# A decode attention block whose keys are scored three ways: 32 of a tile's 256 positions by TensorE's transposes, none summed by ScalarE, and VectorE's multiplication in two parts

## The chip, the cores and the metric

The kernel runs on one core of one Trainium2 chip. The metric is the device time of one execution in microseconds (us). It was run three times: 668.6, 667.44 and 668.81 us, so the median is 668.6 us. One more execution, recorded by the hardware profiler, took 667.49 us; its span, from the first to the last instruction, is 665.8 us. All durations below are from that execution.

## What is computed

One decode step of a transformer block for two sequences: layer norm, attention over a cache of 8,192 positions in 32 heads of 128 elements, and a gated layer behind it. Nearly all bytes are the two caches, 2 x 32 x 8,192 x 128 bf16 values each.

```
q = layernorm(x) @ wq                                   # 2 x 32 heads x 128
scores = einsum("bhqd,bhkd->bhqk", q, k) * 128 ** -0.5  # k: 2 x 32 x 8192 x 128
o = einsum("bhqk,bhkd->bhqd", softmax(scores), v)
h = x + o.reshape(2, 1, 4096) @ wo
out = h + glu(layernorm(h))                             # W_gate, W_up, W_down
```

## The kernel before

**Tiles.** There are 16 steps (`N`), one for four heads of one sequence. Partition 32 j + r of a step holds 256 consecutive positions of head j, so a tile of keys, K(i), is 128 partitions x 256 positions x 128 elements, 8.39 MB, and a tile of values, V(i), is laid out alike. A "position" below is one of the 256 in each partition. There are three such buffers. `load_v(i)` writes V(i) into the buffer that held K(i), once that tile's scores are finished, and `load_k(i + 1)` writes into the buffer of V(i - 2), once the value products of step i - 2 are done. All these loads are issued on SyncE's queue, in the order V(i - 1), K(i + 1), V(i), K(i + 2) and so on (L145).

**The scores of a tile** (`scores`, L331) are made in three ways:
- By VectorE: `mult` (L341) multiplies positions in place by the query, repeated over the partitions. Then the 128 products of each position are added in halves, 128 to 64, 32, 16 and 8 (L412), and a last reduction adds the 8 (L416).
- By ScalarE: `sum_up` (L345 to L350) takes positions that VectorE has multiplied and adds up each one's 128 products, one activation with an accumulator for each position (`NACT`: 48 a tile, 32 in the last).
- By TensorE: `transposed` (L352) transposes 8 positions at a time, and `by_columns` (L359) has ScalarE copy them from PSUM to the tile `kT` (L362) and then multiplies each with the query columns (L364). There is one `kT`, and there are two PSUM tiles for transposed keys, so the transposes of the third chunk follow the products of the first. `scores_of` (L372) copies these scores into the column tile. `NPE` is the number of these positions: none in the first tile, 16 in a middle one, 32 in the last.

**Softmax and values.** `best(i)` (L310) reduces the scores of each partition to their maximum and spreads it with a matmul on TensorE (L314). `powers(i)` (L319) reduces that to the negative maximum on VectorE (L323, tile `nm`) and then has ScalarE make four exponentials (L326) into `pgz`, the weights for the values. It is called in the middle of `scores(i + 1)`. `values(i)` (L433) multiplies `pgz` with V(i): two matmuls written out (L427), and then a loop of 31 rounds of two matmuls each on TensorE (L451 to L453) for the steps 0 to 12. The steps 13 to 15 are written out. `collect` (L461) copies the result of a loop, and `turn` (L469) turns the results of four steps at a time.

**What sets the order.** The order on TensorE, VectorE, ScalarE and SyncE is that of the program text (`manual_schedule`). In a middle step, VectorE multiplies 16 positions (`FIRST`), then 176 (`MIDDLE`), makes the negative maximum of the step before, multiplies the last 48, and adds. ScalarE sums 16 positions, copies the value product of step i - 2, copies two chunks of transposed keys, makes the exponentials of step i - 1, copies the column scores and sums 32 positions. TensorE transposes 16 positions, makes their products and then runs the loop of step i - 1. The first loop's head is placed on slot 169 of an instruction block (`LOOP_AT`, L450); the later ones stand where the code between them puts them.

**The end.** When the scores of the last tile are done, the output and gated-layer weights are loaded into its buffer (L500 to L518), behind the two halves of V(15) in the queue. The rest of the block follows.

Of the kernel before, what the change touches and what calls it, by code (L numbers as in the profile page):

```python
# [7 lines left out]
ACT = mybir.ActivationFunctionType  # L8
ALU = mybir.AluOpType
AXIS = mybir.AxisListType  # L10
# [3 lines left out]
def _free(t, offset, dims):  # L14

    return bass.AP(tensor=t.tensor, offset=t.offset + offset, ap=[t.ap[0]] + [list(d) for d in dims])
# [7 lines left out]
def kernel(  # L24
# [13 lines left out]
    nc = tc.nc  # L38
    P = nc.NUM_PARTITIONS
    B, Sq, D = A_x.shape  # L40
    _, Hkv, Sk, Dh = A_k_cache.shape
# [6 lines left out]
    NT = H4 * Sk // P  # L48
# [2 lines left out]


    TPC = 8
    FIRST = 16
    MIDDLE = 176
    T4 = 4

# [8 lines left out]
    f32 = mybir.dt.float32  # L66
# [19 lines left out]
    ps = ctx.enter_context(tc.tile_pool(name="ps", bufs=1, space=PSUM))  # L86
# [7 lines left out]
    N = len(steps)  # L94
# [40 lines left out]
    hc = consts.tile([P, B, KC], f32)  # L135

    COLS = N - 3
    NACT = {i: 32 if i == N - 1 else 48 for i in range(N)}
    NPE = {i: 0 if i == 0 else 32 if i == N - 1 else 16 for i in range(N)}

    def load_kv(cache, t, i, pieces=1):
        b, g = steps[i]
# [27 lines left out]
    with tc.manual_schedule(engines=ORDERED):  # L170
# [42 lines left out]
        for c in range(KC):  # L213
            nc.tensor.matmul(
                out=x_ps[:, c, :], lhsT=xrow[0:B, bass.DynSlice(c, P, step=KC)], rhs=ident[0:B, 0:B],
# [13 lines left out]
            out=xn.rearrange("p c b -> p b c"), in0=dev, in1=_free(rstd, 0, [[1, B], [0, KC]]), op=ALU.mult,  # L229
# [101 lines left out]
        def scores(i):  # L331
            b, g = steps[i]
            last = i == N - 1
            kt = buf[k_at[i]]
            nmul = NT - NPE[i]
            na = NACT[i]
            scol = scols[i] = small.tile([P, NT], f32, tag=f"scol{i % 2}", name="scol")

            def mult(t0, t1):
                kv = _free(kt, t0 * Dh, [[Dh, t1 - t0], [1, Dh]])  # L340
                nc.vector.tensor_tensor(  # L341
                    out=kv, in0=kv, in1=_free(qrep[b], g * Dh, [[0, t1 - t0], [1, Dh]]), op=ALU.mult,
                )

            def sum_up(t0, t1):  # L345
                for t in range(t0, t1):
                    whole = ps.tile([P, Dh], f32, tag="acc", name="whole")
                    nc.scalar.activation(  # L348
                        out=whole, in_=kt[:, t * Dh:(t + 1) * Dh], func=ACT.Copy, accum_out=scol[:, t:t + 1],
                    )  # L350

            def transposed(c0):  # L352
                t_ps = ps2.tile([P, TPC, P], bf16, tag="tp", name="t_ps")
                for k in range(TPC):
                    t = nmul + c0 + k
                    nc.tensor.transpose(t_ps[:, k, :], kt[:, t * Dh:(t + 1) * Dh], ident)  # L356
                return t_ps

            def by_columns(t_ps):  # L359
                sc_ps = ps.tile([P, NPE[i], H4], f32, tag="sc", name="sc_ps")  # L360
                for c0 in range(0, NPE[i], TPC):
                    nc.scalar.activation(out=kT, in_=t_ps.pop(0).rearrange("p t s -> p (t s)"), func=ACT.Copy)  # L362
                    for t in range(TPC):
                        nc.tensor.matmul(  # L364
                            out=sc_ps[:, c0 + t, :], lhsT=kT[:, t * P:(t + 1) * P],
                            rhs=_free(qT, H4 * g * B + b, [[B, H4]]), start=True, stop=True,
                        )
                    if c0 + 2 * TPC < NPE[i]:
                        t_ps.append(transposed(c0 + 2 * TPC))
                return sc_ps  # L370

            def scores_of(sc_ps):  # L372
                for j in range(H4):
                    r = slice(j * QP, (j + 1) * QP)
                    nc.scalar.activation(out=scol[r, nmul:NT], in_=sc_ps[r, :, j], func=ACT.Copy)  # L375

            left = []
            if i == 0:
                for t0 in range(0, NT, NT // 4):
                    mult(t0, t0 + NT // 4)  # L380
                sum_up(0, na)
            elif last:
                mult(0, nmul)
                scores_of(by_columns([transposed(c0) for c0 in (0, TPC)]))
                sum_up(0, na)
                values(i - 1)
            else:
                mult(0, FIRST)
                if i == 1:
                    powers(i - 1)  # L390
                mult(FIRST, FIRST + MIDDLE)
                t_ps = [transposed(c0) for c0 in (0, TPC)]
                sum_up(0, FIRST)
                if i >= 2:
                    collect(i - 2)
                sc_ps = by_columns(t_ps)
                if i >= 2:
                    powers(i - 1)
                    turn(i - 2)
                left = waiting[:]  # L400
                values(i - 1)
                tc.no_sync_barrier()
                load_k(i + 1)
                scores_of(sc_ps)
                mult(FIRST + MIDDLE, nmul)
                sum_up(FIRST, na)
            n = nmul - na
            width = Dh
            while width > 8:
                half = width // 2  # L410
                lo = _free(kt, na * Dh, [[Dh, n], [1, half]])
                nc.vector.tensor_tensor(  # L412
                    out=lo, in0=lo, in1=_free(kt, na * Dh + half, [[Dh, n], [1, half]]), op=ALU.add,
                )
                width = half
            nc.vector.tensor_reduce(  # L416
                out=scol[:, na:nmul], in_=_free(kt, na * Dh, [[Dh, n], [1, 8]]), axis=AXIS.X, op=ALU.add,
            )
            for e in left:
                waiting.remove(e)  # L420
                normalise(e)
            best(i)
# [10 lines left out]
        def values(i):  # L433
            v = buf[v_at[i]]
            if i >= COLS:
                sums(i)
                g = steps[i][1]
                for t in range(NT):
                    nc.tensor.matmul(  # L439
                        out=o_of(i)[:, 0, H4 * g:H4 * (g + 1)],  # L440
                        lhsT=v[:, t * Dh:(t + 1) * Dh], rhs=pgz[:, H4 * t:H4 * (t + 1)],
                        start=(t == 0), stop=(t == NT - 1),
                    )
                return

            made[i] = ps.tile([P, T4 * Dh], f32, tag="po", name="po")
            with tc.tile_critical(sync_engine=PE):  # L447
                products(i, 0, LOOP)

                at = {PE: LOOP_AT} if i == 0 else None  # L450
                with nc.Fori(1, NT // T4 // LOOP, 1, engines=[PE], head_slot=at) as w:  # L451
                    for u in range(LOOP):
                        nc.tensor.matmul(  # L453
                            out=made[i][0:H4 * T4, :],
                            lhsT=pgz[:, bass.ds((w * LOOP + u) * (H4 * T4), H4 * T4)],
                            rhs=v[:, bass.ds((w * LOOP + u) * (T4 * Dh), T4 * Dh)],
                            start=False, stop=True, skip_group_check=True,
                        )
# [36 lines left out]
        for (h0, m, blocks, k, loads), n in zip(SETS, rows):  # L495
            r0 = h0 * Dh
            for p0, w in blocks:
                r = 0
                for nr in loads:
                    nc.sync.dma_start(  # L500
                        out=wo_sb[p0:p0 + w, off + r * D:off + (r + nr) * D],
                        in_=_dram(A_wo, (r0 + r) * D, [[n * D, w], [1, nr * D]]),
# [9 lines left out]
        for w in WD:  # L512
            nc.sync.dma_start(  # L513
                out=wd2[:, k0:k0 + w, :],
                in_=_dram(B_W_down, k0 * 2 * P * D, [[2 * D, P], [2 * P * D, w], [1, 2 * D]]),
# [12 lines left out]
        for k, (h0, m, blocks, _, _) in enumerate(SETS):  # L528
            n = rows[k]
# [3 lines left out]
            for b in range(B):  # L533
# [4 lines left out]
                for p0, w in blocks:  # L538
                    mb = w // q
                    nc.vector.tensor_tensor(  # L540
                        out=_free(sp, p0, [[q, mb], [1, q]]), in0=_free(ocol, h1 * B + b, [[B, mb], [0, q]]),
                        in1=_free(quot[k], 0, [[0, mb], [1, q]]), op=ALU.mult,
# [4 lines left out]
        for k, (h0, m, blocks, _, _) in enumerate(SETS):  # L547
            n = rows[k]
            pn = sum(blocks[-1])
            for r in range(n):  # L550
                for c in range(KC):
                    nc.tensor.matmul(
                        out=att_ps[:, c, :],
# [18 lines left out]
            out=hx, in0=_free(hc, 0, [[1, KC], [KC, B], [0, PARTS]]), in1=_free(part, 0, [[0, KC], [0, B], [1, PARTS]]),  # L572
            op=ALU.mult,
# [21 lines left out]
        for c in range(KC):  # L595
            nc.tensor.matmul(
                out=y_ps[0:B * PARTS, bass.DynSlice(c, P // PARTS, step=KC)],
# [8 lines left out]
        for r, f in parts:  # L606
            nf = f.stop - f.start
            nc.vector.scalar_tensor_tensor(
                out=gate[r, f, :], in0=g_ps[r, f, :], scalar=0.0, in1=_free(rvar[r], 0, [[0, nf], [1, B]]),
# [8 lines left out]
        for fc in range(FC):  # L618
            w, src = (P, wd_sb[:, fc, :]) if fc < FULL else (LASTW, wd_r[0:LASTW])
            for c in range(KC):  # L620
                nc.tensor.matmul(  # L621
                    out=d_ps[:, :, c], lhsT=src[:, c * P:(c + 1) * P], rhs=hm[0:w, fc, :],
# [4 lines left out]
            out=d, in0=_free(d_ps, 0, [[1, B * KC], [0, KC]]), in1=_free(quarter, 0, [[0, B * KC], [1, KC]]), op=ALU.mult,  # L627
        )
        nc.tensor.matmul(  # L629
            out=y_ps[0:B * PARTS, :], lhsT=d.rearrange("p c q -> p (c q)"), rhs=rest[0], start=False, stop=True,  # L630
# [33 lines left out]
```

## Time and profile before

| what | value |
|---|---|
| three runs, median | 668.6 us (667.44 to 668.81) |
| profiled execution | 667.49 us, span 665.8 us |
| busy: TensorE, VectorE, ScalarE | 366.8, 507.8, 419.9 us |
| moved by DMA | 281.45 MB, 423 GB/s over the span |
| VectorE, multiplication (L341) of 16, 48 and 176 positions | 1.225, 3.349, 11.884 us |
| VectorE, adding of 192 positions (L412, L416) | 6.558, 3.358, 1.757, 0.958 and 1.753 us |
| ScalarE, one position summed (L348), two records | 281 and 186 ns |
| ScalarE, one copy of transposed keys (L362) | 1,024 ns |
| ScalarE, one exponential (L326), two records | 859 and 249 ns |

Busy time is the time in which an engine had an instruction under way. A line of the page or of an answer of the trace that starts with a line number (L341) is a group of instructions: engine, operation, what it writes and reads, how many, then busy time and the mean duration in ns, and behind the bar the idle time ahead of them and what ended it. A line with an arrow (`SPq L145 <- DVE scol L416: 330.8, 15, 31.1`) is a wait: who waited for whom, the total in us, how often, and the longest. DVE is VectorE, ACT ScalarE, PE TensorE, SPq the queue that SyncE issues DMAs from. Lines of a timeline start with the start time and the duration in us. Of the DMA queues, q1 carries the loads; q8 and q14 carry instructions.

### The profile page before, as it was taken

The page shows a single profiled execution, that of the slowest core. Times are in us where ns is not written, and L with a number is a line of the kernel's source. Part 1 is how long each engine was busy: PE and PEld are TensorE (multiplying, and loading weights), DVE is VectorE, ACT ScalarE, POOL GpSimd, SP SyncE. Part 2 cuts the span into 40 slices and gives each one's busy share as a digit, 9 for nine tenths or more (in the row PEclk, how much of TensorE's full clock was granted, in tenths as well). Part 3 has the DMA queues.
Part 4 walks back from the last instruction along what each step waited for, and adds up shares of the span by engine and source line. Part 5 has one row for each costly group of instructions (what it writes and reads, how often), then busy time and mean ns, then how long its engine had stood idle before and what let it go on. Part 6 is the DMA issues. An engine that isn't in the chain of part 4 may idle for free. (4 is left out here: it accounts for less than half of the span.)

```text
span 665.8 us, 10067 instructions
## 1 busy us (share of the span) xinstructions
PE 366.8 (55%) x2601; PEld 148.8 (22%) x2601; DVE 507.8 (76%) x192; ACT 419.9 (63%) x1766; POOL 8.4 (1%) x51
## 2 busy tenths in 40 slices
PE   2601574747647474664638657473865667543456
PEld 1201111111211221121112212111221131242456
DVE  0799969597795959879595996959689595987911
ACT  2596848487594848749475784848669465883720
POOL 5000000000000000000000000000000000000000
PEclk9955696988969798896978979698896979955555
DMA  8999999999999999999999999999999998999996
GB/s 369 448 441 441 434 441 406 426 437 434 441 437 438 434 433 418 433 434 434 437 438 429 425 426 429 423 409 437 426 433 418 425 407 367 429 443 439 414 416 260
DMA packets 6933, 281.45 MB, mean 423 GB/s; under 512 B 786, under 2 KB 884, under 8 KB 1524
## 3 DMA queue, kind: packets, MB, share of 16 engines
q1 hardware_dynamic: 6896, 281.06, 98.5%
q8 instruction: 15, 0.25, 0.1%
q14 instruction: 18, 0.15, 0.1%
q10 hardware_dynamic: 4, 0.00, 0.0%
HBM read 281.05 MB, written 0.00 MB: 422 GB/s over the span
## 5 line engine op out<-in xcount | busy, mean ns | idle before, releaser
L341 DVE TENSOR_TENSOR buf<-buf,qrep 128x2048 bf16<-128x2048 bf16 (+4 forms) x47 | 262.0, 5600 | 104.2 <-DMA buf<-in_A_k_cache_dram 104.2
L453 PE MATMUL po<-buf,pgz 128*16 x806 | 264.7, 408 | 87.8 <-issue 87.6
L348 ACT ACTIVATE whole<-buf 128x128 f32<-128x128 bf16 x752 | 211.4, 281 | 145.3 <-DVE buf L341 122.4
L412 DVE TENSOR_TENSOR buf<-buf 128x12288 bf16<-128x12288 bf16 (+3 forms) x64 | 203.1, 3173 | 2.2
L348 ACT ACTIVATION_READ_ACCUMULATOR whole<-buf 128x1 f32 x752 | 140.2, 186 | 0.2
L453 PEld LDWEIGHTS po<-buf,pgz 128*16 x806 | 72.5, 90 | 285.1 <-issue 241.6
L326 ACT ACTIVATE pgz<-scol,nm 32x256 bf16<-32x256 f32 x64 | 55.0, 859 | 14.0 <-DVE nm L323 10.4
L427 PE MATMUL po<-buf,pgz 128*16 128x512 bf16 x26 | 13.3, 614 | 85.4 <-ACT whole L348 83.0
L362 ACT ACTIVATE kT<-t_ps 128x1024 bf16<-128x1024 bf16 x32 | 32.8, 1024 | 18.9 <-PE t_ps L356 9.7
L439 PE MATMUL o_ps<-pgz,buf 128*128 128x4 bf16 x768 | 21.6, 166 | 20.5 <-DMA buf<-in_A_v_cache_dram 14.6
L364 PE MATMUL sc_ps<-qT,kT 128*128 128x4 bf16 x256 | 11.5, 167 | 38.1 <-ACT kT L362 38.1
L416 DVE TENSOR_REDUCE scol<-buf 128x192 f32<-128x1536 bf16 (+1 forms) x16 | 28.2, 1761 | 0.6
L314 PE MATMUL mx_ps<-nscale,pm 128*128 128x128 f32 x32 | 8.3, 345 | 34.0 <-DVE pm L312 29.3
L439 PEld LDWEIGHTS <-buf 128*128 128x128 bf16 x768 | 21.2, 104 | 21.0 <-DMA buf<-in_A_v_cache_dram 14.8
L356 PE MATMUL t_ps<-ident,buf 128*128 128x128 bf16 x256 | 19.6, 236 | 5.9 <-DMA buf<-in_A_k_cache_dram 5.9
L427 PEld LDWEIGHTS po<-buf,pgz 128*16 128x16 bf16 x26 | 1.3, 90 | 86.5 <-issue 86.5
L465 ACT ACTIVATE ob<-po 16x512 f32<-16x512 f32 x13 | 7.6, 587 | 18.2 <-PEq L447 18.2
L356 PEld LDWEIGHTS <-buf 128*128 128x128 bf16 x256 | 17.7, 107 | 6.4 <-DMA buf<-in_A_k_cache_dram 6.2
L364 PEld LDWEIGHTS <-kT 128*128 128x128 bf16 x256 | 8.7, 98 | 42.7 <-ACT kT L362 42.7
L326 ACT ACTIVATION_READ_ACCUMULATOR pgz<-scol,nm 32x1 f32 x64 | 15.9, 249 | 0.0
L314 PEld LDWEIGHTS mx_ps<-nscale,pm 128*128 128x128 f32 x32 | 5.4, 210 | 38.0 <-issue 28.3
L312 DVE TENSOR_REDUCE pm<-scol 128x1 f32<-128x256 f32 x16 | 6.7, 420 | 8.7 <-ACT whole L348 8.4
(88 smaller groups left out, 103.1 us busy)
## 6 DMA issues: line engine op xcount, KB each, us to landing
buf<-in_A_k_cache_dram SPq DMA_DIRECT2D x4, 2048.0 KB, 23.7
buf<-in_A_v_cache_dram SPq DMA_DIRECT2D x2, 4096.0 KB, 41.1
buf<-in_A_wq_dram SPq DMA_DIRECT2D x1, 4096.0 KB, 12.6
buf<-in_A_wo_dram SPq DMA_DIRECT2D x1, 2048.0 KB, 14.6
buf<-in_A_wo_dram SPq DMA_DIRECT2D x2, 1024.0 KB, 18.7
buf<-in_B_W_gate_dram SPq DMA_DIRECT2D x1, 1376.0 KB
buf<-in_B_W_up_dram SPq DMA_DIRECT2D x1, 1376.0 KB, 24.5
buf<-in_B_W_down_dram SPq DMA_DIRECT2D x1, 768.0 KB, 25.9
```

The source lines that it names most:

```text
L314: nc.tensor.matmul(out=mx[i].rearrange("p a b -> p (a b)"), lhsT=_free(pm, 0, [[0, P]]), rhs=nscale, start=True, stop=True,)
L326: nc.scalar.activation(out=_free(pgz[r, :], j, [[H4, NT]]), in_=scol[r, :], func=ACT.Exp, scale=SCALE, bias=nm[r, j:j + 1], accum_out=zc[r ...
L341: nc.vector.tensor_tensor(out=kv, in0=kv, in1=_free(qrep[b], g * Dh, [[0, t1 - t0], [1, Dh]]), op=ALU.mult,)
L348: nc.scalar.activation(out=whole, in_=kt[:, t * Dh:(t + 1) * Dh], func=ACT.Copy, accum_out=scol[:, t:t + 1],)
L356: nc.tensor.transpose(t_ps[:, k, :], kt[:, t * Dh:(t + 1) * Dh], ident)
L362: nc.scalar.activation(out=kT, in_=t_ps.pop(0).rearrange("p t s -> p (t s)"), func=ACT.Copy)
L364: nc.tensor.matmul(out=sc_ps[:, c0 + t, :], lhsT=kT[:, t * P:(t + 1) * P], rhs=_free(qT, H4 * g * B + b, [[B, H4]]), start=True, stop=True,)
L412: nc.vector.tensor_tensor(out=lo, in0=lo, in1=_free(kt, na * Dh + half, [[Dh, n], [1, half]]), op=ALU.add,)
L416: nc.vector.tensor_reduce(out=scol[:, na:nmul], in_=_free(kt, na * Dh, [[Dh, n], [1, 8]]), axis=AXIS.X, op=ALU.add,)
L427: nc.tensor.matmul(out=made[i][0:H4 * T4, :], lhsT=pgz[:, u * H4 * T4:(u + 1) * H4 * T4], rhs=v[:, u * T4 * Dh:(u + 1) * T4 * Dh], start=( ...
L439: nc.tensor.matmul(out=o_of(i)[:, 0, H4 * g:H4 * (g + 1)], lhsT=v[:, t * Dh:(t + 1) * Dh], rhs=pgz[:, H4 * t:H4 * (t + 1)], start=(t == 0) ...
L453: nc.tensor.matmul(out=made[i][0:H4 * T4, :], lhsT=pgz[:, bass.ds((w * LOOP + u) * (H4 * T4), H4 * T4)], rhs=v[:, bass.ds((w * LOOP + u) * ...
```

## The change

The three ways become two: ScalarE sums no position any more. TensorE's part grows from 16 to 32 positions in a middle tile, from none to 24 in the first, from 16 to 48 in the second and from 32 to 40 in the last. VectorE multiplies and adds all others: 232, 208, 224 (middle) and 216 (last) positions. In a middle tile it multiplies 176 positions first, makes the negative maximum of the step before, and multiplies the other 48; in the second tile the negative maximum comes before both parts. `LOOP_AT` and `MIDDLE` stay as they are.

```diff
-    FIRST = 16
     MIDDLE = 176
...
-    NACT = {i: 32 if i == N - 1 else 48 for i in range(N)}
-    NPE = {i: 0 if i == 0 else 32 if i == N - 1 else 16 for i in range(N)}
+    NPE = {i: (24, 48)[i] if i < 2 else 40 if i == N - 1 else 32 for i in range(N)}
...
-            def sum_up(t0, t1):
-                for t in range(t0, t1):
-                    whole = ps.tile([P, Dh], f32, tag="acc", name="whole")
-                    nc.scalar.activation(
-                        out=whole, in_=kt[:, t * Dh:(t + 1) * Dh], func=ACT.Copy, accum_out=scol[:, t:t + 1],
-                    )
...
             if i == 0:
                 for t0 in range(0, NT, NT // 4):
-                    mult(t0, t0 + NT // 4)
-                sum_up(0, na)
+                    mult(t0, min(t0 + NT // 4, nmul))
+                scores_of(by_columns([transposed(c0) for c0 in (0, TPC)]))
             elif last:
                 mult(0, nmul)
                 scores_of(by_columns([transposed(c0) for c0 in (0, TPC)]))
-                sum_up(0, na)
                 values(i - 1)
             else:
-                mult(0, FIRST)
                 if i == 1:
                     powers(i - 1)
-                mult(FIRST, FIRST + MIDDLE)
+                mult(0, MIDDLE)
                 t_ps = [transposed(c0) for c0 in (0, TPC)]
-                sum_up(0, FIRST)
...
                 scores_of(sc_ps)
-                mult(FIRST + MIDDLE, nmul)
-                sum_up(FIRST, na)
-            n = nmul - na
+                mult(MIDDLE, nmul)
...
-                lo = _free(kt, na * Dh, [[Dh, n], [1, half]])
+                lo = _free(kt, 0, [[Dh, nmul], [1, half]])
```

The adding in halves and the last reduction then run over positions 0 to `nmul` instead of `na` to `nmul`.

More of the change, by code (lines that the diff above doesn't have):

```diff
@@ L335, in scores @@
             nmul = NT - NPE[i]
-            na = NACT[i]
             scol = scols[i] = small.tile([P, NT], f32, tag=f"scol{i % 2}", name="scol")
@@ L410, in scores @@
                 half = width // 2
-                lo = _free(kt, na * Dh, [[Dh, n], [1, half]])
+                lo = _free(kt, 0, [[Dh, nmul], [1, half]])
                 nc.vector.tensor_tensor(
-                    out=lo, in0=lo, in1=_free(kt, na * Dh + half, [[Dh, n], [1, half]]), op=ALU.add,
+                    out=lo, in0=lo, in1=_free(kt, half, [[Dh, nmul], [1, half]]), op=ALU.add,
                 )
@@ L416, in scores @@
             nc.vector.tensor_reduce(
-                out=scol[:, na:nmul], in_=_free(kt, na * Dh, [[Dh, n], [1, 8]]), axis=AXIS.X, op=ALU.add,
+                out=scol[:, 0:nmul], in_=_free(kt, 0, [[Dh, nmul], [1, 8]]), axis=AXIS.X, op=ALU.add,
             )
```

## The prediction

> **What bounds the kernel now.** First the page: the busy tenths, the DMA queues, and the groups that the change touches.
>
> ```profile
> DMA  8999999999999999999999999999999998999996
> ...
> q1 hardware_dynamic: 6896, 281.06, 98.5%
> q8 instruction: 15, 0.25, 0.1%
> q14 instruction: 18, 0.15, 0.1%
> ...
> L348 ACT ACTIVATE whole<-buf 128x128 f32<-128x128 bf16 x752 | 211.4, 281 | 145.3 <-DVE buf L341 122.4
> ...
> L348 ACT ACTIVATION_READ_ACCUMULATOR whole<-buf 128x1 f32 x752 | 140.2, 186 | 0.2
> ```
>
> The 16 DMA engines are busy nearly all the time; VectorE (76%) and ScalarE (63%) are not. Next the waits: of all engines, then the DMA queue's own.
>
> ```profile
> DVE buf L341 <- DMA buf<-in_A_k_cache_dram: 104.2, 18, 7.6
> ...
> DVE pm L312 <- ACT whole L348: 8.4, 12, 3.0
> ```
>
> ```profile
> SPq L145 <- DVE scol L416: 330.8, 15, 31.1
> SPq L145 <- PEq L447: 216.1, 13, 20.8
> ```
>
> VectorE waits for keys, 7.5 us a tile. The queue does wait (V for the end of the scores, the next K for the end of the value loop), but with an earlier transfer still running. So what matters is how fast one load of 8.39 MB goes through.
>
> The trace's DMA records answer that: each load has 16 completion marks, one per engine. First, fifteenth and last mark, in us: K(3) 128.79, 130.75, 131.02; K(9) 361.03, 362.98, 366.66; K(10) 399.75, 401.68, 406.07; K(12) 478.99, 481.08, 484.97; second half of V(15) 638.83, 641.17, 642.30. Up to K(10) the first mark steps by exactly 19.35 a load. **One engine falls behind alone**, and the tile waits for it. Its steps are 19.35 or 20.03 us. Those of 20.02 to 20.04 (to 209.79, 307.92, 347.30, 484.97, 524.37) each hold one 8,192-byte instruction fetch on q14 (at 201.4, 294.7, 343.7, 471.9, 513.7); those of 19.35 to 19.37 (to 189.75, 327.26, 366.66, 464.95, 504.33) hold none. These fetches come after every 111 to 142 records of ScalarE, 128 on average: its instruction stream, 1,814 records, reloaded beside the keys, 0.68 us each time, always on the same engine. From K(10) on the other fifteen are held back too: V is issued 31.5 us after the late engine's mark, by when they have run dry. So the pair of loads takes 39.37 us, not 38.70.
>
> By the Trainium skill, Runtime: NRT & Kernel Launch, section Instruction fetch mechanics, crossing an instruction block costs one bump of a DMA tail, mostly hidden. The trace disagrees by 0.68 us a fetch on the engine that ends last. By that rule the fetches would not be the cause; this is rival 2.
>
> **The change, part by part** (middle tiles; span 665.8 us, 667.49 with what lies around it).
>
> ScalarE: 48 sums go, every 0.433 us (281 and 186 ns, overlapping): 20.8 us a tile, but off the path, since they end 0.45 us after VectorE's reduction (437.14, 437.59). What counts is the stream: 752 x 2 = 1,504 records go, about 40 come (two copies a tile, 1.02 us each, and those of the first tiles). About 350 stay, three fetches instead of thirteen.
>
> VectorE: multiplications 1.225 + 11.884 + 3.349 become 11.884 + 3.349 us (-1.2). The adding goes from 192 to 224 positions. By its rows, 192 cost 6.558 + 3.358 + 1.757 + 0.958 + 1.753 = 14.38, 208 (first tile) 15.52; 224 is then 16.65 (+2.3). Net +1.0; less the 0.45 of waiting for ScalarE, V is issued 0.6 us later. It hides behind K: for tile 2, data of V issued at about 124.2 begin 1.6 to 2.6 later (398.18 to 399.75, 437.58 to 440.3), the first engine is free at 128.8. Cover 2 us; uncovered, the fifteen pay it and the last engine only beyond their spread.
>
> TensorE: 16 more transposes and 16 more column products a tile. They and two more copies stand in front of the exponentials on ScalarE, and so in front of the value loop. The last tile of before already runs four chunks, at half clock:
>
> ```profile
> 603.97 1.02 ACT L362 ACTIVATE kT<-t_ps 128x1024 bf16<-128x1024 bf16 x1 [3.03 <-PE t_ps L356]
> 605.80 1.02 ACT L362 ACTIVATE kT<-t_ps 128x1024 bf16<-128x1024 bf16 x1 [0.81 <-PE sc_ps L364]
> 607.34 1.02 ACT L362 ACTIVATE kT<-t_ps 128x1024 bf16<-128x1024 bf16 x1 [0.52 <-PE sc_ps L364]
> 608.89 1.02 ACT L362 ACTIVATE kT<-t_ps 128x1024 bf16<-128x1024 bf16 x1 [0.52 <-PE sc_ps L364]
> ```
>
> One chunk every 1.53 to 1.55 us (1.83 the first time there). From the end E of a value loop: first copy E + 1.55 in nearly every tile, four copies to E + 7.2, four exponentials at 0.88 to E + 10.7, first product 1.02 later (loop 11 to 12: exponentials end at 544.71, product 545.73), then 27.25 to the next E. That makes **38.97 us a tile**. Before, the exponentials ended at about E + 7.7 and the loop waited until E + 11 for V. This chain is 0.27 slower than the 38.70 of two loads, 3.5 us over 13 tiles. The cover: K(3) was issued at 101.83, and with 1.9 to the data it was 5.7 ahead of the first engine (109.43). VectorE's negative maximum needs E + 1.1; it comes to it 11.9 after K, now 1.2 earlier, and in tile 2 E is 9.4 after K, so 1.4 us are spare; from tile 9 on it waits, by 1.4 us in tile 14, and V's cover shrinks to about 0.9. Carried through tile by tile, nothing empties the DMA engines.
>
> The value loop's place: ScalarE's fetches give 64 bytes an instruction (8,192 / 128), so TensorE's, of 16,384, hold 256. The kernel puts the first loop head on slot 169 of a block (L61, L450). In the trace a body has 10 instructions, and heads are 97 apart, 98 at first, 117 where the turned products lie. Loop 11 then starts at 1,278, slot 254, the only body over a block's end; it takes 1.034 us a round, the others 0.884 to 0.891. That made 4.65 us, let VectorE wait 1.0, V(13) come late, and the fifteen engines idle at 559. With 64 more a tile, heads fall on 75, 237, 142, 67, 228, 133, 38, 219, 124, 29, 190, 115: none straddles (247 to 255 would).
>
> TensorE's own fetches grow by three up to the tail; those at 222.9 and 315.0 pushed one engine back by 1.5 us each, a different one each time, so they widen the spread only.
>
> The edges: in the first tile 24 fewer multiplied (-1.66), 24 more added (+1.70); tile 1 loses 1.1 as the maximum now waits for TensorE uncovered, and V(0) lands only at 72.6; in the last tile -0.54 + 1.70, and the weights' loads still find V(15) running (released 632.6 now, about 626 then, V(15) until 634). Five chunks there lie beside VectorE's 30 us. All nothing.
>
> **Sum.** Unheld, the first marks go on from 399.75 by 12 x 19.35 to 631.95, where 638.83 stood: -6.88. Last minus first at the end was 3.31; after, between 1.95 (the other fifteen up to K(10)) and 3.45 (one push of 1.5 on the latest of them). I take 2.9: -0.4. Together **-7.3 us**; the 20.1 us of weights behind V(15) move along. From 667.49: 660.2. The median shown, 668.6, stands 1.1 above the profiled run; I put the forecast between, 660.7, and 659 to 662.5 as this case's own range.
>
> **Rivals.**
> 1. A value loop straddles after all, or the chain is 0.1 to 0.5 longer. One such loop adds 4.65, of which the remaining cover takes 3: about +1.6; two, +6. Each 0.1 in the chain beyond 0.2 adds 1.2. For it: my count of waits may be off by an instruction or two a tile; loop 2 is ten slots away. 662 to 667. Chance 0.14.
> 2. The late engine is late for another reason than ScalarE's fetches. Then its 39.37 a pair stays, the chain hides in it, and only loop 11 goes, 0.4 us on that engine (20.43 instead of 20.03 to K(14)): 667 to 668.5. Against it: ten steps out of ten agree. Chance 0.07.
> 3. Slower: chunks three and four do not overlap. If their transposes (8 at 55 ns and 0.22 to the end) ran after the previous products, not under the copy, each would cost 2.3 instead of 1.53, and the chain 40.5: 13 x 1.8 = 23 less about 6.5 of cover, 16 us behind the loads, so 9 slower than before, about 676. It is even where the exponentials end at E + 11.6 and slower beyond. For it: the 1.83 above; against: 1.54 and 1.55 behind it, at half clock. Chance 0.08, 669 to 678.
>
> **Chances.** Forecast 0.66, rivals 0.14, 0.07, 0.08, better than 659 0.05. Range 658.5 to 666.8, which holds the forecast, most of rival 1 and some of the rest. About 0.2% (1.3 us) is what a measurement of this kernel can tell from no change. Faster beyond that 0.84, within 0.07, slower 0.09.
>
> **What would show it.** Right: two or three 8,192-byte fetches of ScalarE after the start; last marks of K 38.7 apart, within 3.5 us of the first; four copies 1.53 apart, exponentials ending at E + 10.7, loop ends 38.9 to 39.0 apart; all loops at 0.88 a round; V(15) landing near 635. Wrong: one engine still falling behind with few fetches (rival 2); value loops at 39.5 or more and the DMA engines empty before a K or V is issued (1, 3); a loop at 1.03.

## The result, and the profile after

The changed kernel takes 662.24 us (median of four runs, 662.04 to 662.34), the kernel before 668.54 us beside it (667.44 to 668.81). The ratio is 0.9909, with a 95% interval of 0.9891 to 0.9926. The profiled execution took 662.14 us where that of before took 667.49; its span is 660.4 us. The forecast was 660.7 us, 1.5 us too low, and the time lies inside the range.

The functions stand elsewhere in the changed file: the multiplication is L338, the adding L397 and L401, the copy of transposed keys L352, the exponentials L324, the negative maximum L321, the value loop L438, its copy L450. The page of the changed kernel, first the DMA engines' busy tenths and the queues, then the copies:

```profile
PE 405.6 (61%) x3145; PEld 177.2 (27%) x3145; DVE 523.0 (79%) x178; ACT 153.0 (23%) x300; POOL 8.3 (1%) x51
...
DMA  8999999999999999999999999999999999999996
...
q1 hardware_dynamic: 6896, 281.06, 98.8%
q8 instruction: 19, 0.31, 0.2%
q14 instruction: 7, 0.06, 0.0%
...
L352 ACT ACTIVATE kT<-t_ps 128x1024 bf16<-128x1024 bf16 x66 | 67.5, 1023 | 38.1 <-PE sc_ps L354 25.6
```

ScalarE's busy time falls from 419.9 to 153.0 us and its share from 63 to 23%; TensorE and VectorE become busier (366.8 to 405.6 and 507.8 to 523.0 us). None of that is the gain. The rows that belong to it are the queues': q14, which carries ScalarE's instructions, has 7 packets instead of 18, and q8, TensorE's, has 19 instead of 15. The loads themselves are the same, 281.06 MB in 6,896 packets, and the DMA engines stay at nine tenths to the end.

The waits of the changed kernel, of VectorE and then of the DMA queue:

```profile
DVE buf L338 <- DMA buf<-in_A_k_cache_dram: 89.6, 18, 6.6
```

```profile
SPq L143 <- DVE scol L401: 328.4, 15, 31.1
SPq L143 <- PEq L432: 220.9, 13, 17.7
```

VectorE still waits for keys, 89.6 us instead of 104.2, and no longer for ScalarE's sums: `DVE pm <- ACT whole` is gone. The queue waits about as long as before for its two releasers. So the kernel is bound as before, by the loads; what differs is how fast one goes through. ScalarE in one middle tile (start, duration, operation, and the idle time ahead of it), where the last branch of the value loop came at 413.17 (taken as the loop's end here and below):

```profile
413.67 0.59 ACT L450 ACTIVATE ob<-po 16x512 f32<-16x512 f32 x1 [27.97 <-PEq L432]
414.63 1.02 ACT L352 ACTIVATE kT<-t_ps 128x1024 bf16<-128x1024 bf16 x1 [0.38 <-PE t_ps L346]
416.16 1.02 ACT L352 ACTIVATE kT<-t_ps 128x1024 bf16<-128x1024 bf16 x1 [0.51 <-PE sc_ps L354]
417.69 1.02 ACT L352 ACTIVATE kT<-t_ps 128x1024 bf16<-128x1024 bf16 x1 [0.51 <-PE sc_ps L354]
419.22 1.02 ACT L352 ACTIVATE kT<-t_ps 128x1024 bf16<-128x1024 bf16 x1 [0.51 <-PE sc_ps L354]
420.27 0.86 ACT L324 ACTIVATE pgz<-scol,nm 32x256 bf16<-32x256 f32 x1
...
422.90 0.86 ACT L324 ACTIVATE pgz<-scol,nm 32x256 bf16<-32x256 f32 x1
```

Four copies stand 1.53 us apart, the first 1.46 after the loop's end; the exponentials end at 423.76, 10.6 after it. The loop ends run from 101.47 to 568.92 over twelve tiles, 38.95 each, and every loop takes 0.884 to 0.891 us a round.

The trace's DMA records give each load 16 completion marks, one per DMA engine (first mark, and last minus first, in us):

```
                          before            after
K(10)                     399.75  6.32      400.02  1.69
K(12)                     478.99  5.98      477.44  3.10
second half of V(15)      638.83  3.47      632.37  3.17
last weights              659.08  3.31      652.50  4.53
```

In the changed kernel no engine falls behind tile after tile, and the first mark steps by 19.35 us a load up to V(14), once by 19.48. The first engine ends 6.58 us earlier; the last ends 4.53 behind it instead of 3.31, which takes 1.22 back. Together that is 5.36, and the profiled executions differ by 5.35.

### The profile page after: what moved, and what is told of

Same layout as the page of the kernel before. It is cut to its first block, busy times and chain, and to the rows that moved or that the text cites. A ratio compares the mean times of both kernels' runs of the same rounds, so it can differ in the third digit from the quotient of the medians.

```text
span 660.4 us, 9677 instructions
## 1 busy us (share of the span) xinstructions
PE 405.6 (61%) x3145; PEld 177.2 (27%) x3145; DVE 523.0 (79%) x178; ACT 153.0 (23%) x300; POOL 8.3 (1%) x51
## 3 DMA queue, kind: packets, MB, share of 16 engines
q1 hardware_dynamic: 6896, 281.06, 98.8%
## 5 line engine op out<-in xcount | busy, mean ns | idle before, releaser
L438 PE MATMUL po<-buf,pgz 128*16 x806 | 269.5, 411 | 78.6 <-issue 78.2
L338 DVE TENSOR_TENSOR buf<-buf,qrep 128x22528 bf16<-128x22528 bf16 (+5 forms) x33 | 242.9, 7362 | 89.6 <-DMA buf<-in_A_k_cache_dram 89.6
L397 DVE TENSOR_TENSOR buf<-buf 128x14336 bf16<-128x14336 bf16 (+7 forms) x64 | 233.1, 3642 | 2.2
L438 PEld LDWEIGHTS po<-buf,pgz 128*16 x806 | 73.1, 91 | 280.1 <-issue 252.3
L450 ACT ACTIVATE ob<-po 16x512 f32<-16x512 f32 x13 | 7.6, 585 | 368.2 <-PEq L432 368.2
L352 ACT ACTIVATE kT<-t_ps 128x1024 bf16<-128x1024 bf16 x66 | 67.5, 1023 | 38.1 <-PE sc_ps L354 25.6
L324 ACT ACTIVATE pgz<-scol,nm 32x256 bf16<-32x256 f32 x64 | 55.0, 860 | 51.5 <-DVE nm L321 27.3
L354 PE MATMUL sc_ps<-qT,kT 128*128 128x4 bf16 x528 | 23.8, 167 | 53.7 <-ACT kT L352 53.7
L346 PE MATMUL t_ps<-ident,buf 128*128 128x128 bf16 x528 | 42.7, 236 | 9.3 <-DMA buf<-in_A_k_cache_dram 9.3
L346 PEld LDWEIGHTS <-buf 128*128 128x128 bf16 x528 | 35.2, 106 | 9.9 <-DMA buf<-in_A_k_cache_dram 9.7
L354 PEld LDWEIGHTS <-kT 128*128 128x128 bf16 x528 | 18.2, 100 | 64.5 <-ACT kT L352 64.5
L401 DVE TENSOR_REDUCE scol<-buf 128x224 f32<-128x1792 bf16 (+3 forms) x16 | 32.2, 2012 | 0.5
L424 PEld LDWEIGHTS <-buf 128*128 128x128 bf16 x768 | 21.3, 105 | 18.5 <-DMA buf<-in_A_v_cache_dram 10.3
L324 ACT ACTIVATION_READ_ACCUMULATOR pgz<-scol,nm 32x1 f32 x64 | 15.9, 249 | 0.0
L237 PE MATMUL q_ps<-buf,xn 128*2 128x512 bf16 x32 | 10.5, 467 | 4.5 <-DMA buf<-in_A_wq_dram 3.1
L365 ACT ACTIVATE scol<-sc_ps 32x32 f32<-32x32 f32 (+3 forms) x64 | 12.1, 189 | 2.4 <-PE sc_ps L354 1.4
```

Of the source, the lines that this page charges most:

```text
L324: nc.scalar.activation(out=_free(pgz[r, :], j, [[H4, NT]]), in_=scol[r, :], func=ACT.Exp, scale=SCALE, bias=nm[r, j:j + 1], accum_out=zc[r ...
L338: nc.vector.tensor_tensor(out=kv, in0=kv, in1=_free(qrep[b], g * Dh, [[0, t1 - t0], [1, Dh]]), op=ALU.mult,)
L354: nc.tensor.matmul(out=sc_ps[:, c0 + t, :], lhsT=kT[:, t * P:(t + 1) * P], rhs=_free(qT, H4 * g * B + b, [[B, H4]]), start=True, stop=True,)
L397: nc.vector.tensor_tensor(out=lo, in0=lo, in1=_free(kt, half, [[Dh, nmul], [1, half]]), op=ALU.add,)
L401: nc.vector.tensor_reduce(out=scol[:, 0:nmul], in_=_free(kt, 0, [[Dh, nmul], [1, 8]]), axis=AXIS.X, op=ALU.add,)
L424: nc.tensor.matmul(out=o_of(i)[:, 0, H4 * g:H4 * (g + 1)], lhsT=v[:, t * Dh:(t + 1) * Dh], rhs=pgz[:, H4 * t:H4 * (t + 1)], start=(t == 0) ...
```

## The experiments

The theory: the gain is the end of ScalarE's instruction fetches, 0.68 us each on one DMA engine, and the transposes only pay for taking the sums away, by keeping VectorE from becoming the limit. The rivals: the gain is ScalarE's shorter work, or the value loop that no longer straddles a block end, or the transposes themselves. In what follows "the changed kernel" is the 662.24 us one; every ratio is to the kernel before.

**1. The records without the work.** To each middle tile of the changed kernel 96 activations of one element are added that nothing uses.

```diff
                 scores_of(sc_ps)
+                for _ in range(96):
+                    nc.scalar.activation(out=warm, in_=eps_col, func=ACT.Copy)
```

> The changed kernel, with 96 one-element activations of ScalarE added at the end of its part of each middle tile, where it is idle. They compute nothing that is used; 1,344 records, so ten or eleven more 8,192-byte fetches. My theory (ScalarE's instruction fetches keep one DMA engine back): that engine falls behind by 0.68 us a fetch again, about as far as before the change, and the time goes back to 665.5 to 667.5 us. Rival (the gain came from the value loop that no longer straddles, or from VectorE no longer waiting for sums): these are as in the changed kernel, so 662 to 662.7.

Measured: 667.99 us, ratio 0.9994 (0.9985 to 1.0003). The whole gain is gone. The page's rows:

```profile
PE 402.8 (60%) x3145; PEld 177.6 (27%) x3145; DVE 522.6 (78%) x178; ACT 424.2 (64%) x1644; POOL 8.4 (1%) x51
...
q14 instruction: 17, 0.14, 0.1%
```

The fetches are back, at 112.3, 156.6, 198.3, 240.2, 282.0, 323.7, 365.6 and so on. With those from 198.3 to 323.7 the last engine's lag grows from 2.09 over 2.76, 3.45 and 4.13 to 4.80 us, in steps of 0.67 to 0.69, as in the kernel before; from about 380 on the other engines are held back too, and the lag stays between 4.5 and 5.6.

**2. The work without the records.** To each middle tile of the changed kernel 32 long activations are added instead (128 x 512 elements into a PSUM tile that nothing reads).

```diff
+                for _ in range(32):
+                    spare = ps.tile([P, 4 * Dh], f32, tag="acc", name="spare")
+                    nc.scalar.activation(out=spare, in_=_free(qrep[0], 0, [[1, 4 * Dh]]), func=ACT.Copy)
```

> The changed kernel, with 32 activations of 128x512 added at the same place of each middle tile, about 19 us of ScalarE, as much as the sums took, but 448 records instead of 1,344. They compute nothing that is used. My theory: three or four fetches more, on an engine that is not the last one; 661.8 to 663. Rival (ScalarE's busy time or its traffic on the memories slows the loads): back to 666 or more.

Measured: 662.39 us, ratio 0.9909 (0.9893 to 0.9924), as the changed kernel.

```profile
PE 405.0 (61%) x3145; PEld 177.6 (27%) x3145; DVE 522.6 (79%) x178; ACT 421.0 (64%) x748; POOL 8.3 (1%) x51
...
q14 instruction: 10, 0.08, 0.0%
```

Read the two fences against each other: ScalarE is busy for 424.2 and 421.0 us, as in the kernel before, and the times are 5.6 us apart. What differs is 1,644 records against 748, and 17 packets on q14 against 10. (The 10 are three more than in the changed kernel, whose median is 0.15 us lower.) ScalarE's busy time is worth nothing here; the length of its instruction stream is worth the whole change. The Trainium skill, Runtime: NRT & Kernel Launch, section Instruction fetch mechanics, has the cost of crossing an instruction block as mostly hidden. Runs 1 and 2 disagree for ScalarE's fetches in a kernel that its DMA engines bound: they are 5.6 us apart.

**3. The transposes without dropping the sums.** In the kernel before, 32 positions by TensorE in the middle tiles, and ScalarE's 48 sums stay.

```diff
-    NPE = {i: 0 if i == 0 else 32 if i == N - 1 else 16 for i in range(N)}
+    NPE = {i: 0 if i == 0 else 32 for i in range(N)}
```

> The transposes alone: the kernel before, with 32 positions of a middle tile by TensorE instead of 16, and the 48 sums on ScalarE kept. My theory: ScalarE's fetches stay (13 or so), the late engine too; 667 to 669. V is issued some 3 us later, as the sums now start behind four copies, which the late engine hides. Rival (the transposes bring the gain, by relieving VectorE): 662 to 664.

Measured: 669.0 us, ratio 1.0007 (0.9998 to 1.0016). 19 packets on q14. VectorE's busy time falls from 507.8 to 476.9 us and nothing comes of it. The run doesn't isolate the transposes, though: ScalarE's sums now start behind four copies, so V is issued 34.93 us after K has landed in the third tile instead of 31.63, and from there on only 1.3 to 2.7 us ahead of the first engine; that engine too is held back (its first such step is 19.88 us instead of 19.35). That the transposes alone bring nothing is shown better by run 1, which has all of them and none of the gain.

**4. Dropping the sums without the transposes.** In the changed kernel 16 positions by TensorE in every tile but the last, which has 32, so that VectorE multiplies and adds 240 (224 in the last); the first loop head is on slot 140, so that none straddles.

```diff
-    NPE = {i: (24, 48)[i] if i < 2 else 40 if i == N - 1 else 32 for i in range(N)}
+    NPE = {i: 32 if i == N - 1 else 16 for i in range(N)}
```

> The removal of the sums alone: the changed kernel, with 16 positions by TensorE in a middle tile (16 in the first two, 32 in the last), VectorE doing all others, and the first loop's head on slot 140, so that no loop straddles. My theory: ScalarE's stream is short, TensorE's as short as before, so its fetches push fewer engines back; VectorE is 2.3 us longer a tile, just inside the cover: 660 to 662.5. Rival (VectorE's load matters, so that the transposes are needed): 665 or more.

Measured: 667.81 us, ratio 0.9989 (0.9977 to 1.0001). The expectation was wrong. There are six packets on q14, and yet the gain is gone. The DMA queue's waits and VectorE in the third tile, in this run:

```profile
SPq L143 <- DVE scol L401: 380.0, 15, 35.5
```

```profile
108.55 15.73 DVE L397 TENSOR_TENSOR buf<-buf 128x15360 bf16<-128x15360 bf16 x4
124.32 2.15 DVE L401 TENSOR_REDUCE scol<-buf 128x240 f32<-128x1920 bf16 x1
```

The queue's wait for VectorE is 380.0 us, against 328.4 in the changed kernel. V is issued 34.47 us after K has landed instead of 32.27 (37.92 in the second tile), and its first mark comes 19.4 to 20.5 us after the one before it instead of 19.35 (22.27 in the second tile): the engines have run dry. The first engine ends 7.69 us later than in the changed kernel, and 2.92 of them come from the second tile, which has 16 positions by TensorE here and 48 there. How early V must be issued is read off best in runs 11 and 12, by how far its issue lies ahead of the first mark of the load in front of it:

```
V issued ahead by     2.91   2.75   2.64   2.54   2.40   2.39 us
first mark steps by  19.36  19.35  19.45  19.48  19.61  19.71 us
```

In these two runs nothing is lost at 2.75 us or more, and a gap opens at 2.64 or less. Elsewhere the edge is not that sharp. In run 4 itself the steps are 19.36 to 19.92 at 2.2 to 2.7 us ahead and 19.7 to 20.5 at 1.1 to 2.1; in run 6 loads issued 2.51 and 2.53 ahead step by 19.35 and 19.36; and in the kernel before, one issued 1.92 ahead steps by 19.37 and the next four V, at 1.6 to 1.9, by 20.0 to 20.3. The prediction had reckoned with 1.9 us, and this expectation put VectorE just inside the cover.

**5. The straddling loop alone.** The kernel before with the first head on slot 140; no loop straddles.

```diff
-    LOOP_AT = 169
+    LOOP_AT = 140
```

> The kernel before, with the first loop's head on slot 140 instead of 169, so that no later loop straddles the end of a block (loop 11 runs 4.65 us faster). My theory: the late DMA engine sets the time and hardly notices; 0.2 to 1.2 us less than before, 667.3 to 668.3. Rival (the straddling loop cost a good part of the 6 us): 663 to 666.

Measured: 668.46 us against 667.99 for the kernel before, ratio 1.0004 (0.9995 to 1.0013). All loops run at 0.884 to 0.891, loop 11 too. It brings nothing: the first engine ends at 657.81, but the late engine is 5.24 behind.

**6. A straddling loop in the changed kernel.** The first head on slot 187, so that loop 2 lies over a block's end.

```diff
-    LOOP_AT = 169
+    LOOP_AT = 187
```

> The changed kernel, with the first loop's head on slot 187, which puts loop 2's head on slot 252, over the end of a block; the other twelve lie inside a block. My theory: loop 2 at 1.03 us a round, 4.65 us late; the chain of TensorE and ScalarE (38.95 a tile) never catches up with the loads (38.70), so later tiles find V issued late: 0.5 to 2.5 us more, 662.7 to 664.7. Rival (the cover takes all of it): 662.0 to 662.5. Other rival (a straddle does not matter here): all loops at 0.885.

Measured: 665.14 us, ratio 0.9964 (0.9952 to 0.9976), 2.9 us more than the changed kernel and a little more than expected. Loop 2 takes 1.034 us a round, all others 0.884 to 0.887. Its 4.6 us are never caught up: the loop of tile 12 ends at 573.60 instead of 568.92, and the tiles between stay 38.9 to 39.0 apart. From K(4) on V is issued 34.2 to 35.8 us after K. The first engine ends 4.4 us later (656.88), while the idle moments let the late ones catch up (2.60 behind instead of 4.53).

**7. Five chunks.** 40 positions by TensorE in the middle tiles, head on slot 160.

```diff
-    NPE = {i: (24, 48)[i] if i < 2 else 40 if i == N - 1 else 32 for i in range(N)}
+    NPE = {i: (24, 48)[i] if i < 2 else 40 for i in range(N)}
```

> The changed kernel, with 40 positions of a middle tile by TensorE: five chunks (first loop's head on slot 160, no straddle). VectorE has 8 positions less. My theory: the exponentials end at E + 12.1, the chain takes 40.5 us a tile, 1.8 more than two loads, 22 us over the tiles, of which some 7 are covered: 673 to 679, and the DMA engines run empty before loads of K or V. Rival (the copies are not on the path, VectorE is): 660 to 662.

Measured: 678.51 us, ratio 1.0153 (1.0139 to 1.0168). ScalarE in a middle tile of this run:

```profile
426.85 1.02 ACT L352 ACTIVATE kT<-t_ps 128x1024 bf16<-128x1024 bf16 x1 [0.38 <-PE t_ps L346]
428.38 1.02 ACT L352 ACTIVATE kT<-t_ps 128x1024 bf16<-128x1024 bf16 x1 [0.51 <-PE sc_ps L354]
...
433.01 1.02 ACT L352 ACTIVATE kT<-t_ps 128x1024 bf16<-128x1024 bf16 x1 [0.52 <-PE sc_ps L354]
...
434.06 0.86 ACT L324 ACTIVATE pgz<-scol,nm 32x256 bf16<-32x256 f32 x1
```

The fifth chunk costs the 1.53 us that each of the others costs. The exponentials end 12.15 after the loop and the loop ends are 40.5 apart, beyond the 38.70 of two loads. From K(7) on K is issued only 0.6 to 1.5 us ahead, and its load steps by 19.9 to 20.8. The chain through ScalarE's copies is then what bounds the kernel.

**8. Three chunks.** 24 positions in the middle tiles of the changed kernel.

```diff
-    NPE = {i: (24, 48)[i] if i < 2 else 40 if i == N - 1 else 32 for i in range(N)}
+    NPE = {i: (24, 48)[i] if i < 2 else 40 if i == N - 1 else 24 for i in range(N)}
```

> The changed kernel, with 24 positions of a middle tile by TensorE: three chunks; first, second and last tile as they are. VectorE has 8 positions more, V is issued about 33.4 us after K instead of 32.3, still 3.5 ahead of the first engine's need; the chain is 37.4 us; TensorE's stream is 32 instructions a tile shorter, one or two fetches less. My theory: 660.8 to 662.5. Rival (VectorE's 1.1 us is no longer covered, as in the run without more transposes): 664 or more.

Measured: 662.0 us, ratio 0.9909 (0.9895 to 0.9923). The exponentials end 9.06 after the loop, V is issued 33.37 after K and still 3.25 to 3.46 ahead. Three chunks and four give the same time: with two VectorE is late (run 4), with five TensorE and ScalarE are (run 7), and between them only the loads count.

**9 and 10. Fewer instructions of TensorE behind the last keys.** The value products of step 13 are made in the loop too, to spare TensorE fetches and so the spread at the end; run 10 has three chunks in the middle tiles besides. The collecting copy is called ahead of the turn.

```diff
-    COLS = N - 3
+    COLS = N - 2
...
         powers(N - 2)
+        collect(N - 3)
         turn(N - 3)
```

> The changed kernel with the value products of step 13 too made in the loop (32 rounds of 4) instead of 128 single products; some 370 fewer instructions of TensorE behind K(15), so one or two of its 16,384-byte fetches fewer while V(15) and the weights are loaded. Theory (the spread of the last marks, 4.53 us instead of the 2.9 that were predicted, comes from these fetches): the first engine's last mark stays at about 652.5, the spread falls to 3.0 to 3.5, the time to 660.3 to 662. Rival (the spread has another cause): spread 4.5 and 662.2. Second rival: the loop's 27 us stand where the single products took less, V(15) or the weights are issued too late and the engines run dry: 663 or more.

> As the run with the loop for step 13, and with three chunks (24 positions) by TensorE's transposes in the middle tiles instead of four; 16 more instructions of TensorE fewer in each tile. Theory: the two do not hinder each other, spread 3.0 to 3.5, 660.2 to 661.8. If VectorE's cover for V (3.3 us ahead of the first engine) is already too little with the value loop in step 13: 662.5 to 664.

Measured: 682.41 us, ratio 1.0211 (1.0197 to 1.0224), and 678.12 us, ratio 1.0148 (1.0135 to 1.0161). Both missed. VectorE in run 9:

```profile
590.65 0.42 DVE L310 TENSOR_REDUCE pm<-scol 128x1 f32<-128x256 f32 x1
609.21 0.29 DVE L321 TENSOR_REDUCE nm<-mx_ps 128x4 f32<-128x128 f32 x1 [18.14 <-PE mx_ps L312]
616.11 0.31 DVE L301 RECIPROCAL rz<-o_ps 128x24 f32<-128x24 f32 x1 [6.61 <-PE o_ps L293]
616.45 0.18 DVE L302 TENSOR_TENSOR ocol<-o_ps,rz 128x24 bf16<-128x24 f32 x1
616.55 14.55 DVE L338 TENSOR_TENSOR buf<-buf,qrep 128x27648 bf16<-128x27648 bf16 x1
```

And in the changed kernel:

```profile
591.68 0.29 DVE L321 TENSOR_REDUCE nm<-mx_ps 128x4 f32<-128x128 f32 x1 [0.89 <-PE mx_ps L312]
...
596.79 14.56 DVE L338 TENSOR_TENSOR buf<-buf,qrep 128x27648 bf16<-128x27648 bf16 x1 [4.39 <-DMA buf<-in_A_k_cache_dram]
```

Two things hold VectorE back. The matmul that spreads the maximum of step 14 stands behind the products of step 13 on TensorE; behind the loop it starts at 608.72 instead of 590.84, so the negative maximum comes at 609.21 instead of 591.68. Then VectorE waits another 6.61 us for the turned results of step 13, which need the loop's result, and ScalarE copies that only behind its exponentials. VectorE, in its own order, can't start on K(15) before both: 616.55 instead of 596.79, 19.8 us, nearly the whole loss of 20.2. The weights, which wait for K(15)'s scores, come late, and the DMA engines run dry: the weights' first mark stands 22.22 us behind V(15)'s instead of 4.87. Run 10 has the same two waits (15.68 and 6.88 us), and VectorE starts on K(15) at 614.29. The second rival of run 9 had the longer loop and the empty engines, without a size ("663 or more"); neither expectation looked at who is queued behind the loop. The runs say nothing on the spread that they were made for.

**11 and 12. Other fetch times.** The changed kernel with the first loop head on slot 109, or 227, so that TensorE's block ends come 60 instructions later or 58 earlier. No loop straddles.

```diff
-    LOOP_AT = 169
+    LOOP_AT = 109
```

> The changed kernel with the first value loop's head on slot 109 instead of 169, so that every later block end of TensorE's stream comes 60 instructions later and meets other loads, with no loop over a block's end. Nothing else changes: first engine's last mark 652.5 as before. Theory: which engine a fetch pushes, and so the spread at the end, changes, between 2 and 5 us; time 660 to 663. Rival (the spread is a property of the loads' order): spread 4.4 to 4.6 and 662.0 to 662.4.

> As the run with slot 109, with the head on slot 227: block ends come 58 instructions earlier than in the changed kernel, no loop over one. First engine's last mark 652.5. Theory: spread between 2 and 5 us, not 4.5 again except by accident; time 660 to 663. Rival: spread 4.4 to 4.6 and 662.0 to 662.4.

Measured: 662.38 us, ratio 0.9922 (0.9903 to 0.9941; five of six runs lie between 662.19 and 662.40, one at 666.32), and 662.17 us, ratio 0.9908 (0.9893 to 0.9922). The last engine ends 4.30 and 4.60 behind the first. That a fetch hits an engine by accident, which both expectations called the theory, is not what the runs show; with the fetches at other times the spread stays nearly the same. What it does depend on comes out of all the runs' DMA records, by the number of the fetch (from the start, at 28 us; times and the last engine's lag in us):

```
                 9th fetch  lag around it    17th fetch  lag around it
changed kernel   461.6      1.80 -> 3.10     643.3       3.3 -> 4.6
slot 109         422.8      1.96 -> 3.25     638.5       2.9 -> 4.1
slot 227         459.1      1.95 -> 3.2      639.7       3.4 -> 4.7
three chunks     570.4      2.07 -> 3.14     651.5       3.5 -> 4.5
```

The lag of the last engine jumps with the 9th and the 17th fetch, whenever these come. If each packet is joined to the one that ended 3 or 4 ns after its start, the 16 engines can be told apart for long stretches. In the changed kernel, the 9th to 12th and the 14th to 16th fetch then fall on the engines of the 1st to 4th and the 6th to 8th; in the run with three chunks, the 9th to 12th on those of the 1st to 4th; in run 11, the 17th on that of the 9th. So TensorE's fetches seem to go over eight of the 16 engines in turn, and each round pushes the latest one by 0.9 to 1.3 us more. Some other pairs don't match in this count, where two engines end within a few ns and their chains can be swapped; the turn by eight is inferred from both views, not shown for every fetch. Where the loads had left gaps before, the 9th fetch shows no such jump (run 6, at 466.4: 1.80 to 1.85).

## Why the prediction came out as it did

**What bounds the kernel: right.** The loads bind, one DMA engine fell behind alone, and ScalarE's instruction fetches were the cause. The prediction had this from ten steps of one trace; runs 1 and 2 show it by making the fetches come back without the work and the work without the fetches. The rival that the fetches are not the cause has fallen: its 667 to 668.5 us is what run 1 gives, with the fetches back.

**The chain through the transposes: right.** Copies 1.53 apart (1.53 to 1.55 predicted), exponentials ending 10.6 behind the loop (10.7), 38.95 us a tile (38.97). VectorE waits for the maximum from tile 9 on, as worked out, but only in the tiles 9, 10 and 11 (0.31, 0.49 and 0.61 us). In the tiles 12 to 14 it doesn't wait, where the prediction had 1.4 us for the last: K lands later there, because the last engine's lag has grown to 3.1 us. The rival of a straddling loop or a longer chain has fallen, since no loop straddles. The rival with chunks that don't overlap has fallen too; run 7, where a fifth chunk makes the chain as long, shows what it would have cost: 40.5 us a tile and 678.5 us, against 40.5 and about 676 by the prediction.

**The first engine's end: right.** -6.88 predicted, for V(15)'s second half and all behind it. Its first mark came at 632.37 instead of the 631.95 predicted, which is -6.46, and the last weights' is at -6.58.

**The spread: the step that failed.** "After, between 1.95 and 3.45 (one push of 1.5 on the latest of them). I take 2.9: -0.4." It was 4.53, +1.22. Of the 1.94 us between the 660.2 worked out for the profiled execution and its 662.14, this makes 1.63 and the first engine 0.30. The prediction took TensorE's fetches to push "a different one each time" and allowed one push on the latest engine. The runs point to a turn by eight: with 19 fetches the latest engine is pushed in the second round and again in the third. The kernel before, with 15, has no third round ahead of its end. By this a changed kernel with at most 16 fetches ahead of the last weights should end about 1 us earlier; that is an estimate from the jump at the 17th. Runs 9 and 10 were meant to come near that and failed for another reason, so it stays untried.

**The straddling loop: size wrong, without effect on the forecast.** The prediction put loop 11 at 0.4 us where it goes alone, in its second rival; run 5 shows no gain that can be measured. In the changed kernel one straddling loop was priced at +1.6 us and cost 2.9 (run 6), since nothing later makes up for it.

**The cover of V: too generous.** It was costed at nothing, and nothing was lost: V was issued at least 3.24 us ahead. But the margin to the 2.75 us that were still enough in run 11 is 0.5, not the 0.9 that the prediction saw, and run 4 fell over this edge.

## What to carry to other kernels

In a kernel that the DMA engines bind, count instruction records as well as bytes: an engine that is far from its limit can still cost time by the length of its instruction stream, and the completion marks of the single DMA engines show it where averages do not. When an edit takes work off an idle engine and gives it to the two others, ask first for how long each of them stays covered: here two chunks were too few, five too many, and three or four the same. Before something is moved, write down who stands behind it in the same engine's order; run 9 lost 20 us to small matmuls that stood behind a loop.

## What the runs showed of the hardware that was not expected

- ScalarE's fetches of 8,192 bytes came once in about 128 records and cost the engine that they ran on 0.68 us each, in the kernel before and in run 1.
- TensorE's fetches of 16,384 bytes seem to go over eight DMA engines in turn, 0.9 to 1.3 us a push on the latest one; the 9th and 17th widened the spread in each of four kernels whose loads left few gaps.
- In runs 11 and 12 a load had to be issued about 2.7 us ahead of the first engine's end for its data to follow without a gap (2.75 ahead: 19.35 us a load; 2.40 ahead: 19.61); in other runs 2.3 to 2.5 were sometimes enough, and once 1.92.
- A value loop over the end of an instruction block took 1.034 us a round in place of 0.884, with two matmuls in a round, and this held for all 30 rounds.
